# Weight conversion from double to single precision: the sign carried by a Prelu slope in place of two kinds of sign pass

## The chip, the cores and the metric

The kernel runs on one core of one Trainium2 chip. The core has a matrix engine (TensorE, PE in the profile; PEld is its loading of weights), a vector engine (VectorE, DVE), a scalar engine (ScalarE, ACT), GpSimd (POOL) and SyncE (SP), which here does nothing but issue DMAs. The metric is the device time of one execution in microseconds (us). Three runs of the kernel before gave 1497.77 us as the median, 1496.57 and 1499.21 us as the ends.

## The reference, cut to what matters

```python
def _attn_ref(q, k, v, p):
    p_packed = sm_attn(p, k, v)              # 32 packed tokens per head attend to 576
    return sm_attn(q, p_packed, p_packed)    # 576 tokens per head attend to the 32

def _moe_ref(x, w_in, w_out):                # x: 4608 x 512, d_ff 2048
    h = x @ w_in
    g = h - np.tanh(h)
    return (g @ w_out).astype(np.float32)

def _moe2_ref(x, w_in, w_out):
    h = x @ w_in
    g = h * np.cos(h)
    return (g @ w_out).astype(np.float32)

def reference(**kwargs):                     # 8 batches, 8 heads, 576 tokens, width 64
    attn_out = _attn_ref(...)
    x = heads put side by side, one row for each token
    return _moe2_ref(_moe_ref(x, ...), ...)
```

The four weight matrices are double precision (float64). The kernel gets them as 64-bit words and has to make single-precision words of them on the chip. That conversion is all that the change touches.

## The kernel before, in words

**Stages.** There are 8 batches of 576 tokens, handled as 16 half-batches of 288 tokens. The first feed-forward layer with its attention is a row of 128 steps, numbered n = 0 to 127. A step takes two of the 16 column groups of `w_in` for one half-batch: `h1` (L508) does twelve matmuls into a PSUM tile `h`, `el1` and `el2` (L529, L535) compute g = h - tanh(h) on ScalarE and VectorE, `el3` and `el4` split g into a high and a low half, and `ymm1` (L568) multiplies the g of two steps earlier by the `w_out` groups, 24 matmuls. The `h` tile has two buffers, and VectorE's L545 is the last that reads one. Attention of the next batch is spread over the steps as pieces (`early`, `mid`, `quick`), and so is `gmat` with `gsplit` (L470, L489), which multiplies the packed attention rows by converted `w_in` groups and splits the product `g`: the high half on ScalarE (L493), the low half on VectorE (L498). After step 127 there is one 512-token tile of the second layer done plainly (`h2`), and then four passes over pairs of tiles in a scheme with fewer products (`hprod`, `yprod`, L900, L910).

**Weight conversion.** `Conv` (L131 to L253) has three parts. `a` takes a staged tile `st` of 128 x 512 doubles. `hi` is each upper 32-bit word and `x` each lower one. L167 reads `hi` as a single and multiplies it by 2^-112, which leaves the right exponent in the wrong place (three bits too far right). L170 scales the lower word to a small integer. `b` then shifts the word left by three and ors the low bits in (`join`, L208, VectorE). The shift pushes the sign bit out, so the sign has to be put into `x` beforehand, and this is done in one of two ways, read letter by letter from `SPLIT` (first layer) and `SPLIT2` (second layer): for "S" ScalarE writes a half-precision number with the right sign over the upper half of `x` (L175), for "L" VectorE ands the sign out of `hi` and ors it into `x` (L187). `c` splits a converted tile into a high half on ScalarE (L231) and a low half on GpSimd (L232); of the first layer only `w_out` tiles go through it.

**Where the conversions stand.** There are 32 tiles for each layer. The first layer's are converted in the prologue and in steps 0 to 21 (`STEP_A` says how many calls of `a` a step makes); `SPLIT` has 12 "S" and 20 "L". The second layer's are converted in steps 34 to 126 (`CONV2`), all but the last 8 the "S" way.

**Order.** The first part of the prologue (to L1004) and everything from step 15 on stands in a manual schedule, that is in program order. Between them, in steps -16 to 14, Tile's planner orders each engine's queue from the program, by priority and by its own estimate of when things are ready. Loads of staged tiles are issued by `prefetch` (L144) on SP's queue, after a `join` has freed a slot of the pool `wp`.

Of the kernel before, what the change touches and what calls it, by code (L numbers as in the profile page):

```python
# [14 lines left out]
U16 = mybir.dt.uint16  # L15
U32 = mybir.dt.uint32
F16 = mybir.dt.float16
BF16 = mybir.dt.bfloat16
AF = mybir.ActivationFunctionType
ALU = mybir.AluOpType  # L20
# [13 lines left out]
    "i2 i0 i3 i1 o1 o0 i4 i5 i6 i7 o3 o4 o2 o5 o7 i8 "  # L34
    "o6 i9 i10 i11 i14 o9 i12 i13 o8 i15 o11 o13 o12 o10 o15 o14"
).split()
SPLIT = "LLSSLLSLLLSLSLSLLSLSLSLSLLSLLSLL"
SPLIT2 = "S" * 24 + "L" * 8
STEP_A = (1, 2, 2, 2, 1, 2, 1, 1, 1, 1, 0, 2, 1, 1, 1, 1, 1, 1, 0, 3, 1, 1)
CONV2 = (34, 35, 37, 38) + tuple(16 * k + r for k in (3, 4, 5, 6) for r in (0, 2, 3, 5, 6))  # L40
CONV2 += (112, 114, 116, 118, 120, 122, 124, 126)
# [29 lines left out]
    11: (13,), 12: (12, 14), 13: (15, 18, 16), 14: (19,), 16: (17,), 17: (20, 21), 18: (22,),  # L71
}
PREP0 = (23, 24, 25)
SGN = -2147483648
LOW_BIAS = -0.5 + 2.0 ** -10


# [1 line left out]
def fused_kernel(ctx, tc, qT, kT, v, pT, w1i, w1o, w2i, w2o, ident, out):  # L79
    nc = tc.nc  # L80
    B, _, _, _, HB = qT.shape
    S = 2 * HB
# [36 lines left out]
    def f32(ap):  # L119
        return ap.bitcast(F32)  # L120
# [10 lines left out]
    class Conv:  # L131
# [20 lines left out]
        def a(self):  # L152
            self.prefetch()
            if not self.ready:
                return
            kind, f, st = self.ready.pop(0)
            way = self.split[self.na]
            self.na += 1
            if kind == "w1i":
                if f // 2 not in w1in:  # L160
                    w1in[f // 2] = wp.tile([128, 2, 512], F32, tag="w", name="w1i")
                w = w1in[f // 2][:, f % 2, :]
            else:
                w = self.alloc_tmp()
            sv = st.rearrange("p (n two) -> p n two", two=2)
            hi, x = sv[:, :, 1], sv[:, :, 0]
            nc.scalar.activation(out=w, in_=f32(hi), func=AF.Copy, scale=2.0 ** -112)  # L167
            halves = st.bitcast(U16).rearrange("p (n four) -> p n four", four=4)
            if way != "D":
                nc.scalar.activation(  # L170
                    out=x, in_=x.bitcast(U32), func=AF.Identity,
                    scale=2.0 ** -29 * (1 - 2.0 ** -11), bias=LOW_BIAS,
                )
            if way == "S":
                nc.scalar.activation(  # L175
                    out=halves[:, :, 1].bitcast(F16), in_=f32(hi), func=AF.Copy, scale=2.0 ** -60
                )
            self.done_a.append((kind, f, hi, w, x, way))

        def b_ops(self):  # L180
            if not self.done_a:
                return []
            kind, f, hi, w, x, way = self.done_a.pop(0)
            wi = w.bitcast(I32)

            def sign():
                nc.vector.scalar_tensor_tensor(  # L187
                    out=x, in0=hi, scalar=SGN, in1=x, op0=ALU.bitwise_and, op1=ALU.bitwise_or
                )

            def shift():
                nc.vector.tensor_scalar(
                    out=wi, in0=wi, scalar1=3, scalar2=None, op0=ALU.logical_shift_left
                )

            def put_sign():
                nc.vector.scalar_tensor_tensor(
                    out=wi, in0=hi, scalar=SGN, in1=wi, op0=ALU.bitwise_and, op1=ALU.bitwise_or
                )

            def join():
                if way == "D":
                    nc.vector.scalar_tensor_tensor(
                        out=wi, in0=x, scalar=29, in1=wi,
                        op0=ALU.logical_shift_right, op1=ALU.bitwise_or,
                    )
                else:
                    nc.vector.scalar_tensor_tensor(  # L208
                        out=wi, in0=wi, scalar=3, in1=x,
                        op0=ALU.logical_shift_left, op1=ALU.bitwise_or,  # L210
                    )
                if kind == "w1i":
                    self.bdone.add(f)
                else:
                    self.done_b.append((kind, f, w))
                if kind[1] == "2":
                    stores.append((raw[kind[2]][f // 2][:, f % 2], w))
                self.prefetch()

            return {"S": [join], "L": [sign, join], "D": [shift, put_sign, join]}[way]  # L220

        def b(self):
            for fn in self.b_ops():
# [426 lines left out]
    def cos_round(a, h):  # L650
        nc.scalar.activation(out=a, in_=h, func=AF.Identity, bias=MAGIC)

    def cos_frac(a, h):
        nc.vector.scalar_tensor_tensor(
            out=a, in0=a, scalar=MAGIC, in1=h, op0=ALU.subtract, op1=ALU.subtract
        )
# [306 lines left out]

    conv = Conv([("w1" + o[0], int(o[1:])) for o in ORDER], 3, SPLIT, alloc_st, alloc_tmp)

# [74 lines left out]

    conv2 = Conv(todo2, 2, SPLIT2, alloc_st2, alloc_tmp2)

# [25 lines left out]
    for n, (blk, s) in enumerate(steps):  # L1068
# [7 lines left out]
        st = {}  # L1076
# [85 lines left out]
    for s in range(NSTEP):  # L1162
        st = st0 if s == 0 else {}
# [70 lines left out]
    def psp():  # L1234
        i = nbank[0] % 4
        nbank[0] += 1
        if banks[i] is not None:
            t, banks[i] = banks[i], None
            return t
        return psx.tile([128, TB], F32, tag=f"p{i}", bufs=1, name="p")  # L1240
# [78 lines left out]
    for t in pairs:  # L1319
# [23 lines left out]
        for F in range(NSTEP):  # L1343
            w = wfirst if (t, F) == (pairs[0], 0) else None
# [4 lines left out]
            A, C, B = psp(), psp(), psp()  # L1349
# [82 lines left out]
        for k, (p, P) in enumerate(jobs):  # L1432
# [7 lines left out]
            hi, lo = done[k]  # L1440
# [102 lines left out]
```

## Time and profile before

| what | value |
|---|---|
| time, median of 3 runs | 1497.77 us (1496.57 to 1499.21) |
| profiled execution, first to last instruction (span) | 1498.1 us |
| the profiled execution's own time | not given apart from the span; the span lies inside the range of the runs |
| PE busy | 1443.1 us, 96% |
| DVE busy | 1230.8 us, 82% |
| ACT busy | 1034.3 us, 69% |
| POOL busy | 126.6 us, 8% |
| DMA | 307.64 MB, mean 205 GB/s |

Busy times are of one profiled execution. An engine's idle time costs something only where that engine sets the end of its stage, so the table by itself says little: the stages have to be read one by one.

### The profile page before, as it was taken

The page shows a single profiled execution, that of the slowest core. Times are in us where ns is not written, and L with a number is a line of the kernel's source. Part 1 is how long each engine was busy: PE and PEld are TensorE (multiplying, and loading weights), DVE is VectorE, ACT ScalarE, POOL GpSimd, SP SyncE. Part 2 cuts the span into 40 slices and gives each one's busy share as a digit, 9 for nine tenths or more (in the row PEclk, how much of TensorE's full clock was granted, in tenths as well). Part 3 has the DMA queues.
Part 4 walks back from the last instruction along what each step waited for, and adds up shares of the span by engine and source line. Part 5 has one row for each costly group of instructions (what it writes and reads, how often), then busy time and mean ns, then how long its engine had stood idle before and what let it go on. Part 6 is the DMA issues. An engine that isn't in the chain of part 4 may idle for free.

```text
span 1498.1 us, 29038 instructions
## 1 busy us (share of the span) xinstructions
PE 1443.1 (96%) x11296; PEld 1309.5 (87%) x11296; DVE 1230.8 (82%) x1689; ACT 1034.3 (69%) x1592; POOL 126.6 (8%) x102
## 2 busy tenths in 40 slices
PE   4789999999999999999999999999999999999998
PEld 2668888999899899989998888998889888998898
DVE  6999888897988989899986778886888688868874
ACT  5888766879788796887875656655665466636652
POOL 0221101111111112111120000000000000000000
PEclk8799999999999999999999999999999999999999
DMA  9633363645747566473669747787668766777656
GB/s 351 226 122 103 122 210 118 222 138 199 249 140 252 169 210 211 166 245 128 206 257 370 256 159 233 230 256 210 203 188 254 214 207 190 232 240 208 179 162 184
DMA packets 179977, 307.64 MB, mean 205 GB/s; under 512 B 14912, under 2 KB 110144, under 8 KB 179840
## 3 DMA queue, kind: packets, MB, share of 16 engines
q1 hardware_dynamic: 179840, 305.79, 63.2%
q8 instruction: 90, 1.47, 0.4%
q14 instruction: 47, 0.39, 0.1%
HBM read 238.35 MB, written 67.37 MB: 204 GB/s over the span
## 4 chain that ended last, share of the span: by engine, by line
PE 81%; ACT 7%; DVE 5%; issue 3%; DMA 2%; POOL 0%; SPq 0%; DVEq 0%; POOLq 0%; ACTq 0%
PE p L900 21%; PE y L579 20%; PE y L910 14%; PE h L517 10%; PE p L910 6%; PE h L640 3%; PE y L716 3%; PE gp L479 2%; ACT st L175 1%; ACT u L533 1%; DVE y L551 1%; ACT st L170 1%; DMA yw<-wod 1%; DVE d L545 1%; ACT y L539 1%
## 5 line engine op out<-in xcount | busy, mean ns | idle before, releaser
L579 PE MATMUL y<-gh,w1o 128*128 128x288 f32 x2048 | 307.5, 303 | 9.1 <-ACT w1o L231 2.8
L579 PEld LDWEIGHTS y<-gh,w1o 128*128 128x128 f32 x2048 | 280.8, 190 | 38.3 <-ACT t L532 15.3
L900 PE MATMUL p<-b,hw 128*128 128x512 f32 x1302 | 310.4, 391 | 0.0
L900 PEld LDWEIGHTS p<-b,hw 128*128 128x128 f32 x1302 | 239.0, 188 | 47.0
L517 PE MATMUL h<-a,g 128*128 128x288 f32 x1536 | 227.9, 297 | 15.3 <-DVE g L498 7.5
L517 PEld LDWEIGHTS h<-a,g 128*128 128x128 f32 x1536 | 212.7, 190 | 19.1 <-ACT st L170 8.2
L532 ACT ACTIVATE t<-h 128x576 f32<-128x576 f32 x128 | 85.1, 665 | 127.2 <-PE h L517 127.1
L579 PE MATMUL y<-gl,w1o 128*128 128x288 f32 x1024 | 158.5, 297 | 0.0
L579 PEld LDWEIGHTS y<-gl,w1o 128*128 128x128 f32 x1024 | 145.2, 191 | 0.1
L910 PE MATMUL y<-yw,yh 128*128 128x256 f32 x768 | 136.0, 279 | 1.5 <-DMA yw<-wod 1.4
L551 DVE COPY_PREDICATED y<-k,t 128x576 f32<-128x576 int16 x128 | 111.7, 873 | 10.8 <-DVE y L547 0.5
L544 DVE TENSOR_TENSOR t<-h,t 128x576 f32<-128x576 f32 x128 | 95.2, 744 | 29.9 <-ACT u L533 28.9
L910 PEld LDWEIGHTS y<-yw,yh 128*128 128x128 f32 x768 | 117.5, 188 | 2.5 <-ACT o L921 2.0
L564 DVE TENSOR_TENSOR gl<-y,gh 128x576 fp32r<-128x576 f32 x128 | 107.0, 836 | 1.7 <-ACT gh L559 1.6
L910 PE MATMUL y<-yw,yl 128*128 128x256 f32 x384 | 107.3, 279 | 0.0
L918 DVE TENSOR_TENSOR yl<-k,yh 128x1024 fp32r<-128x1024 f32 x72 | 87.0, 1219 | 23.5 <-ACT yh L921 22.9
L547 DVE SCALAR_TENSOR_TENSOR y<-y,d 128x576 f32<-128x576 f32 x128 | 97.0, 758 | 2.4 <-ACT y L539 2.1
L559 ACT ACTIVATE gh<-y 128x576 fp32r<-128x576 f32 x128 | 87.8, 686 | 12.2 <-DVE y L551 11.6
L545 DVE TENSOR_TENSOR d<-u,h 128x576 f32<-128x576 f32 x128 | 95.0, 742 | 0.0
L910 PE MATMUL y<-yw,gh 128*128 128x256 f32 x512 | 94.0, 280 | 0.0
L910 PE MATMUL p<-yw,yh 128*128 128x256 f32 x512 | 91.0, 279 | 0.0
L921 ACT ACTIVATE c<-p 128x512 f32<-128x512 f32 x96 | 56.9, 593 | 49.2 <-PE p L900 49.2
(164 smaller groups left out, 2580.6 us busy)
## 6 DMA issues: line engine op xcount, KB each, us to landing
yw<-wso SPq DMA_DIRECT2D x128, 256.0 KB, 3.1
hw<-wsi SPq DMA_DIRECT2D x124, 256.0 KB, 3.1
w1i<-w1d SPq DMA_DIRECT2D x48, 512.0 KB, 5.1
yw<-wod SPq DMA_DIRECT2D x96, 256.0 KB, 3.3
hw<-wid SPq DMA_DIRECT2D x93, 256.0 KB, 3.3
y<-ye SPq DMA_DIRECT2D x80, 144.0 KB, 1.9
st<-w1i SPq DMA_DIRECT2D x16, 512.0 KB, 8.4
v<-vv SPq DMA_DIRECT2D x16, 512.0 KB, 6.5
```

What stands on the lines that cost most here:

```text
L517: nc.tensor.matmul(out=h[:, x, 0:HB], lhsT=gw[b, f // 4, half][:, ga, c0:c0 + 128], rhs=a2[b, half][:, aa, HB * j:HB * j + HB], start=(n = ...
L532: nc.scalar.activation(out=st["t"], in_=h, func=AF.Tanh)
L544: lambda: nc.vector.tensor_tensor(out=t, in0=hs, in1=t, op=ALU.subtract),
L545: lambda: nc.vector.tensor_tensor(out=d, in0=u, in1=hs, op=ALU.mult),
L547: lambda: nc.vector.scalar_tensor_tensor(out=y, in0=y, scalar=PC0 - PC1 * PC1 / (4 * PC2), in1=d, op0=ALU.add, op1=ALU.mult,),
L551: lambda: nc.vector.copy_predicated(out=y, mask=k.bitcast(I16), data=t),
L559: nc.scalar.activation(out=st["gh"], in_=st["g"], func=AF.Copy)
L564: nc.vector.tensor_tensor(out=st["gl"], in0=st["g"], in1=f32(st["gh"]), op=ALU.subtract)
L579: nc.tensor.matmul(out=yps[blk][d][:, 0:HB], lhsT=w1out[f][:, wh, 128 * d:128 * d + 128], rhs=st[gg][:, x, :], start=(s in first and x == ...
L900: nc.tensor.matmul(out=dst, lhsT=w[:, wi, 128 * j:128 * j + 128], rhs=b[j][bi], start=(first and n == 0), stop=(n == 5), skip_group_check= ...
L910: nc.tensor.matmul(out=dst[m // 2][:, 256 * (m % 2):256 * (m % 2) + 256], lhsT=src[:, 128 * m:128 * m + 128], rhs=w[:, wi, :], start=(firs ...
L918: nc.vector.tensor_tensor(out=out, in0=x, in1=y, op=op)
```

## The change

The multiplication at L167 becomes a Prelu with the same scale and with a slope of 2^32 for negative numbers. A negative word thus gets an exponent larger by 32, and that bit of the exponent field is the one that the later shift by three moves into the place of the sign. So no sign has to be put into `x`: the half-precision write on ScalarE (L175) and the and-or on VectorE (L187) are gone, and every tile is converted by L167, L170 and the join. All 32 + 32 tiles take this way (letter "A"); another way, "V", is defined and not used. The low half of `g` (L498) stays on VectorE. Nothing else is edited: `STEP_A`, `CONV2`, the order of tiles, the pools and the loads are as they were.

```diff
-SPLIT = "LLSSLLSLLLSLSLSLLSLSLSLSLLSLLSLL"
-SPLIT2 = "S" * 24 + "L" * 8
+SPLIT = "A" * 32
+SPLIT2 = "A" * 32
...
             hi, x = sv[:, :, 1], sv[:, :, 0]
-            nc.scalar.activation(out=w, in_=f32(hi), func=AF.Copy, scale=2.0 ** -112)
-            halves = st.bitcast(U16).rearrange("p (n four) -> p n four", four=4)
-            if way != "D":
+            nc.scalar.activation(
+                out=w, in_=f32(hi), func=AF.Prelu, scale=2.0 ** -112, alpha=2.0 ** 32
+            )
+            if way == "A":
                 nc.scalar.activation(
                     out=x, in_=x.bitcast(U32), func=AF.Identity,
                     scale=2.0 ** -29 * (1 - 2.0 ** -11), bias=LOW_BIAS,
                 )
-            if way == "S":
-                nc.scalar.activation(
-                    out=halves[:, :, 1].bitcast(F16), in_=f32(hi), func=AF.Copy, scale=2.0 ** -60
-                )
...
-            def sign():
-                nc.vector.scalar_tensor_tensor(
-                    out=x, in0=hi, scalar=SGN, in1=x, op0=ALU.bitwise_and, op1=ALU.bitwise_or
-                )
...
-            return {"S": [join], "L": [sign, join], "D": [shift, put_sign, join]}[way]
+            return {"A": [join], "V": [shift, join]}[way]
```

## Rows read from the trace of the kernel before

**Rows 1.** The page: busy time of each engine, and slices of the span.
```profile
PE 1443.1 (96%) x11296; PEld 1309.5 (87%) x11296; DVE 1230.8 (82%) x1689; ACT 1034.3 (69%) x1592; POOL 126.6 (8%) x102
...
PE   4789999999999999999999999999999999999998
```

**Rows 2.** Windows by stage: length, busy PE, PEld, DVE, ACT, POOL; granted clock, DMA.
```profile
14.00:35.00 21.00, 9.20 (x162) 4.03 (x154) 17.80 (x35) 14.68 (x24) 0.00 (x0) 0.77 1.04 394
35.00:110.00 75.00, 60.39 (x513) 49.06 (x514) 69.67 (x106) 66.19 (x114) 21.08 (x14) 0.84 0.55 188
110.00:172.00 62.00, 57.73 (x546) 53.21 (x546) 55.56 (x80) 54.06 (x101) 9.58 (x7) 0.99 0.37 117
172.00:700.00 528.00, 518.08 (x5027) 481.04 (x5027) 460.88 (x739) 411.74 (x719) 77.43 (x61) 1.00 0.56 189
700.00:800.00 100.00, 99.02 (x683) 95.10 (x682) 82.69 (x111) 76.04 (x134) 18.16 (x14) 1.00 0.64 227
```

**Rows 3.** Windows, VectorE's sign pass L187 alone: length, busy time and count.
```profile
14.00:35.00 21.00, 1.38 (x2) 0.77 1.04 394
35.00:110.00 75.00, 12.22 (x14) 0.84 0.55 188
110.00:172.00 62.00, 4.49 (x4) 0.99 0.37 117
```

**Rows 4.** Windows, ScalarE's sign pass L175 alone: length, busy time and count.
```profile
35.00:110.00 75.00, 10.92 (x8) 0.84 0.55 188
110.00:172.00 62.00, 2.79 (x2) 0.99 0.37 117
172.00:700.00 528.00, 33.23 (x24) 1.00 0.56 189
```

**Rows 5.** The chain that ended at 172 us, from 14 us: shares by line.
```profile
by line: issue 12.4%; PE y L579 8.8%; DVE y L551 6.9%; PE h L517 6.3%; ACT st L175 5.8%; ACT st L170 4.0%; DVE st L187 3.8%; DVE t L544 3.1%; ACT gh L559 2.9%; DVE d L545 2.5%; PE gp L479 2.4%; ACT w1i L167 2.4%; ACT y L539 2.2%; ACT u L533
```

**Rows 6.** Groups of ScalarE, 14 to 172 us: busy, mean ns, idle before.
```profile
L175 ACT ACTIVATE st<-st 128x512 f16<-128x512 f32 x12 | 16.4, 1368 | 0.1
...
L532 ACT ACTIVATE t<-h 128x576 f32<-128x576 f32 x20 | 13.1, 657 | 10.3 <-PE h L517 10.3
L542 ACT ACTIVATE k<-u 128x576 bf16<-128x576 f32 x19 | 13.1, 689 | 0.0
...
L167 ACT ACTIVATE w1i<-st 128x512 f32<-128x512 f32 x16 | 10.7, 683 | 0.0
```

**Rows 7.** Timeline of VectorE near 37 and 88 us: start, duration, line.
```profile
36.70 0.69 DVE L187 SCALAR_TENSOR_TENSOR st<-st 128x512 int32<-128x512 int32 x1
37.30 0.16 DVE L349 RECIPROCAL sm<-sm 128x1 f32<-128x1 f32 x1
...
88.40 1.47 DVE L187 SCALAR_TENSOR_TENSOR st<-st 128x512 int32<-128x512 int32 x1
89.79 0.74 DVE L544 TENSOR_TENSOR t<-h,t 128x576 f32<-128x576 f32 x1
```

**Rows 8.** Timeline of GpSimd near 88 us.
```profile
87.74 1.58 POOL L407 TENSOR_TENSOR u<-u,m 128x576 f32<-128x576 f32 x1 [5.24 <-DVE m L406]
```

**Rows 9.** Waits of TensorE, 35 to 110 us: total, times, longest, us.
```profile
PE h L517 <- DVE g L498: 7.3, 1, 7.3
PE gp L479 <- DVE w1i L208: 3.7, 2, 2.1
```

**Rows 10.** Waits of TensorE, 14 to 35 us.
```profile
PE pt L458 <- DVE px L388: 0.8, 1, 0.8
```

**Rows 11.** Waits of TensorE, 172 to 700 us.
```profile
PE h L517 <- DVE d L545: 3.6, 4, 0.9
```

**Rows 12.** Timeline of ScalarE near 376 us: start, duration, line.
```profile
376.46 1.37 ACT L175 ACTIVATE st<-st 128x512 f16<-128x512 f32 x1
377.57 0.74 ACT L532 ACTIVATE t<-h 128x576 f32<-128x576 f32 x1
```

**Rows 13.** Line L1133: the later of the two table loads of ScalarE (ns).
```profile
L1133 ACT ACT_TABLE_LOAD  x1: 1283/1283/1283, 778.5 to 778.5; - x1
```

More of the change, by code (lines that the diff above doesn't have):

```diff
@@ L73 @@
 PREP0 = (23, 24, 25)
-SGN = -2147483648
 LOW_BIAS = -0.5 + 2.0 ** -10
@@ L194, in shift @@
                 )
[L196 to L199, printed above, removed]
             def join():
-                if way == "D":
+                if way == "V":
                     nc.vector.scalar_tensor_tensor(
```

## The prediction, made before the changed kernel was run

> **What bounds the kernel now.** I read the page first. TensorE is busy 96% of the span and its slices stand at 9 nearly everywhere, but the first three are 4, 7 and 8 [rows 1]. So the kernel is bound by TensorE but for its first 110 us or so, and 32 of the 64 conversions lie there. The windows by stage show what bounds each stretch [rows 2]. From 14 to 35 us and from 35 to 110 us VectorE is the fullest engine (17.80 of 21 us and 69.67 of 75 us), ScalarE is close behind (66.19 of 75), and TensorE has time to spare (60.39 of 75, and part of that at a granted clock of 0.84). From 110 to 172 us all three are nearly full: TensorE 57.73 of 62, so that at most 4.3 us can be won there. From 172 to 700 us TensorE is busy 518.08 of 528 us, and from 700 to 800 us 99.02 of 100: there a pass that is taken from another engine is worth something only where TensorE waits for it. The chain of waits up to 172 us names both passes that the change removes: of its 158 us ScalarE's L175 holds 5.8%, that is 9.2 us, and VectorE's L187 holds 3.8%, 6.0 us [rows 5]. Together 15.2 us: with both gone this chain is that much shorter, and something else may then be late.
>
> **The change part by part.**
>
> *The multiplication as a Prelu.* The trace before has no Prelu. The nearest rows are ScalarE's other functions: in the same stretch Tanh (L532) takes 657 ns and Relu (L542) 689 ns on 576 columns, the copy of L167 itself 683 ns on 512 strided ones [rows 6]. These three differ by 5%, so I take 683 ns, no change. The upper end is the dearest pass of this size, L175 with 1368 ns [rows 6], the lower end the 657 ns of Tanh, 0.03 us a tile less. The Trainium skill, "ScalarE: Activation LUTs", section "Table sets: the hidden batching unit", says that functions come in sets and that a function out of the loaded set needs a table load; its list of the cheap functions that are in every set names relu, copy, identity and abs, and not Prelu. The trace agrees on what one load costs, 1283 ns [rows 13], and shows nothing on Prelu's set. By that rule's bad case the change loses; it is the last rival below.
>
> *ScalarE's sign pass L175.* Twelve stand before 172 us and 24 later [rows 4, 6]. One takes 1.37 us, but the next instruction starts 1.11 us after it [rows 12]; so 1.1 us of ScalarE's time each.
>
> *VectorE's sign pass L187.* 20 stand before 172 us (2, 14 and 4 in the three stretches), 8 after 700 us, where TensorE is full [rows 2, 3]. An undisturbed one holds the queue for 0.60 us (36.70 to 37.30) [rows 7]. The mean is 0.91 us, 18.09 us over 20 [rows 3], since some are much longer: the one at 88.40 takes 1.47 us, and GpSimd's pass from 87.74 to 89.32 lies over most of it [rows 7, 8]. Of such a one I count 0.60 us, since the next pass may have to sit out the same collision. The upper end, all that L187 was busy, stays for the range. The Trainium skill, "SBUF — State Buffer", section "Who interferes with whom", has it that a VectorE instruction with two SBUF inputs and a GpSimd instruction that reads SBUF lock each other out for a whole instruction. By that rule the excess stays whenever the next pass has two such inputs, and goes where it has one (L544 behind the pass at 88.40 reads PSUM); the sum by the rule lies between 8.4 and 12.2 us for the stretch below.
>
> *14 to 35 us.* The prologue's order is manual. TensorE's transpose of the packed rows waits 0.8 us for `px` on VectorE [rows 10], and ahead of `px` stand a sign pass and its join. Gain 0.6 us, one pass; bounds 0 and 0.8. The rest of this stretch is attention on VectorE, which the change doesn't touch.
>
> *35 to 110 us.* VectorE sets the pace: 5.3 us idle of 75 [rows 2]. Fourteen passes by 0.60 us make 8.4 us. ScalarE gets rid of 8 by 1.1 us, 8.8 us, so it doesn't take VectorE's place. TensorE's two long waits here end with VectorE (7.3 us for the low half of `g`, 3.7 us for a join) [rows 9], which fits. Upper bound 12.2 us [rows 3]; lower bound 3 us, the sign passes ahead of the waited-for joins (five of 0.60 us, an estimate), where the planner or the attention chain of the next batch holds the rest. I take 8.4 us: what bounds the stretch loses that much of its queue.
>
> *110 to 172 us.* Four passes of VectorE and two of ScalarE go (2.4 and 2.2 us), TensorE's idle time is 4.3 us [rows 2 to 4]. I take half of the latter, 2.1 us; bounds 0 and 4.3.
>
> *172 to 700 us.* TensorE waits 3.6 us in all for L545, four times 0.9 us [rows 11]. L545 comes behind Tanh on ScalarE, which at 377.57 starts 1.11 us late because an L175 stands ahead of it [rows 12]. The passes gone, Tanh starts up to 1.1 us sooner, and 1.1 is more than 0.9. Gain 3.6 us; bounds 0 (if another wait of the same length stands behind) and 3.6. All else that leaves ScalarE here (24 by 1.1 us) is covered by TensorE, and so are VectorE's 8 passes after 700 us: 0 us, at most the 1.0 us that TensorE is idle there [rows 2].
>
> No DMA, no wait and no buffer is added; staged tiles come free sooner, so their loads go out sooner.
>
> *The sum.* 0.6 + 8.4 + 2.1 + 3.6 = 14.7 us. The span is 1498.1 us, so 1483.4 us; the median of the runs is 0.3 us below the span, so 1483.1 us for the metric. As a cross-check: the first three terms make 11.1 us of the 15.2 us that the chain holds.
>
> **The rivals.**
>
> *The early order keeps part of it.* In steps -16 to 14 the planner lays out the queues anew, and the attention of the next batch passes through VectorE, GpSimd and ScalarE in turn. If that chain sets the pace, the lower bounds hold: 0 + 3 + 1 + 3.6 = 7.6 us, so about 1490 us. For it: 12.4% of the chain up to 172 us is "issue", not work [rows 5]. Against it: VectorE is busy 93% of 35 to 110 us [rows 2].
>
> *All of it comes through.* Collisions leave with the passes, and TensorE fills its gaps: 0.8 + 12.2 + 4.3 + 3.6 + 1.0 = 21.9 us, about 1476 us. Against it: TensorE would have to have no wait at all from 110 us on.
>
> *The loads take over.* The DMA engines are full from 14 to 35 us (share 1.04, 394 GB/s) [rows 2]. If the tiles arrive no sooner than now, the terms up to 110 us are gone, 9.0 us, and 1492 us is left. Against it: from 35 to 110 us the share is 0.55.
>
> *A Prelu that costs more, and the kernel is slower.* ScalarE gets back 12 by 1.1 us, 13.2 us, before 172 us and does 32 Prelus there: it breaks even at 0.41 us more for each, about 1.09 us in all. At L175's 1368 ns it has 32 by 0.69 us, 21.9 us, more and is the bound in place of VectorE: 8.7 us more than before, of which its idle time covers a part, so some 1500 us. If each Prelu switched the table and back, 64 loads by 1.28 us are 82 us; the 13.2 us and ScalarE's idle time of 23.0 us from 14 to 172 us [rows 2] cover 36, and it would be about 1540 us. Against it: the similar cost of three functions [rows 6].
>
> **How the numbers follow.** Forecast (14.7 us, its own range 1479 to 1487) 0.59; early order 0.20; all of it 0.11; loads 0.05; dear Prelu 0.05. The range takes in the second and third: 1476 to 1491.5 us. What a measurement of this kernel can tell from no change is 0.2%, 3.0 us. Forecast and first three rivals all lie more than that below; to fall within 3.0 us the early stages would have to give nothing and the four waits also to stay, for which I take 0.05 out of the first two rivals' share. Faster 0.90, same 0.05, slower 0.05.
>
> **What would show it.** Right: L167 at some 0.68 us, no table load but two; the start of the steady stretch (now 172 us) 9 to 13 us earlier, by VectorE's shorter queue; the four waits for L545 gone; from 800 us on the same length. Wrong: the steady stretch starts where it did, with VectorE idle more than now in 35 to 110 us (then order or loads bound it), or the waits for L545 remain, or L167 is longer.

## The result, and the profile after

The changed kernel takes 1479.46 us (median, 1478.96 to 1480.42); beside it the kernel before took 1497.89 us. The ratio is 0.9875, 95% interval 0.9861 to 0.9889: 18.4 us less, where 14.7 had been forecast. 1483.1 us was predicted, with a range of 1476.0 to 1491.5.

The page of the changed kernel, busy times and the slices of TensorE:

```profile
PE 1434.7 (97%) x11296; PEld 1305.6 (88%) x11296; DVE 1211.8 (82%) x1661; ACT 992.6 (67%) x1556; POOL 127.1 (9%) x102
...
PE   5889999999999999999999999999999999999998
```

VectorE has 28 instructions less and ScalarE 36, exactly the sign passes, and the first three slices of TensorE stand at 5, 8 and 8 instead of 4, 7 and 8 [rows 1]. The windows by stage, columns as in [rows 2]:

```profile
14.00:35.00 21.00, 9.91 (x157) 4.49 (x149) 17.59 (x35) 13.37 (x24) 0.00 (x0) 0.77 1.04 394
35.00:110.00 75.00, 63.66 (x581) 55.52 (x580) 67.78 (x103) 65.25 (x122) 22.95 (x15) 0.91 0.60 211
110.00:172.00 62.00, 59.38 (x599) 54.93 (x598) 52.16 (x79) 49.63 (x94) 9.61 (x7) 1.00 0.34 108
172.00:700.00 528.00, 522.33 (x5049) 486.81 (x5048) 469.97 (x749) 392.45 (x711) 77.71 (x62) 1.00 0.57 192
700.00:800.00 100.00, 100.00 (x631) 93.09 (x630) 75.04 (x99) 70.67 (x115) 16.49 (x13) 1.00 0.75 275
```

From 35 to 110 us VectorE and ScalarE are about as full as before, but the same 75 us hold 581 matmuls instead of 513: the work got denser, not lighter. From 110 us on TensorE's idle time shrinks in each window.

The functions of ScalarE up to the steady stretch (busy us, mean ns, idle before), where L166 is the Prelu:

```profile
L518 ACT ACTIVATE t<-h 128x576 f32<-128x576 f32 x20 | 13.0, 652 | 12.7 <-PE h L503 12.6
L528 ACT ACTIVATE k<-u 128x576 bf16<-128x576 f32 x19 | 13.0, 682 | 0.0
...
L166 ACT ACTIVATE wt<-st 128x512 f32<-128x512 f32 x16 | 10.8, 673 | 1.0 <-DMA st<-w1o 0.9
L166 ACT ACTIVATE w1i<-st 128x512 f32<-128x512 f32 x16 | 10.7, 680 | 0.0
```

A Prelu takes 673 to 680 ns, the copy took 683 [rows 6]. The table loads in the whole span are the two of before:

```profile
L953 ACT ACT_TABLE_LOAD x1 | 1.3, 1283 | 0.7 <-PEq L1519 0.7
L1119 ACT ACT_TABLE_LOAD x1 | 1.3, 1283 | 0.0
```

TensorE's waits from 172 to 700 us:

```profile
PE y L565 <- DVE ye L595: 2.3, 1, 2.3
PE sc L303 <- PE h L503: 1.8, 5, 0.8
PE s L303 <- PE h L503: 1.3, 6, 0.2
PE pt L444 <- DVE g L484: 0.2, 1, 0.2
```

The line that answers to [rows 11], four waits for L545 (now L531), is gone. At the place of [rows 12], Tanh no longer stands behind a sign pass; it waits for TensorE instead:

```profile
361.24 0.69 ACT L170 ACTIVATE st<-st 128x512 int32<-128x512 uint32 x1
362.64 0.65 ACT L518 ACTIVATE t<-h 128x576 f32<-128x576 f32 x1 [0.71 <-PE h L503]
```

Where the time went can be read off the starts of the 128 steps (first matmul of `h1`). The table gives how much earlier a step starts than in the profile before, in us:

| run | step 0 | step 10 | step 17 | step 31 | step 104 | step 127 | end of span |
|---|---|---|---|---|---|---|---|
| after | 1.2 | 9.8 | 11.6 | 13.1 | 18.6 | 18.7 | 19.5 |
| prelu_only | 0.2 | -0.3 | 0.5 | 2.0 | 1.8 | 1.8 | 3.2 |
| no_vector_sign | 0.5 | 4.5 | 5.4 | 5.4 | 5.2 | 5.2 | 7.9 |
| no_scalar_sign | 1.7 | 1.5 | 2.2 | 2.3 | 7.7 | 7.8 | 9.1 |
| second_layer_only | 0.8 | 0.8 | 0.7 | 0.7 | 6.1 | 6.2 | 9.1 |

The last column holds noise of its own. After the steps TensorE meets up to three waits for loads and stores in the last passes, which differ from profile to profile (0.8 and 0.5 us for loads and 0.6 us for ScalarE in the one after, 0.6 and 0.8 us for loads in the one before, one of 0.2 us in prelu_only). A run's own time is 1.8 us above its span (1480.42 against 1478.6 us for the profiled run after), so the profile before, with 1498.1 us, is of a run about 2 us above the median: of the 19.5 us between the two spans about 1 is the choice of runs.

### The profile page after: what moved, and what is told of

Read it like the earlier page. It is cut to its first block, busy times and chain, and to the rows that moved or that the text cites. A ratio compares the mean times of both kernels' runs of the same rounds, so it can differ in the third digit from the quotient of the medians.

```text
span 1478.6 us, 29015 instructions
## 1 busy us (share of the span) xinstructions
PE 1434.7 (97%) x11296; PEld 1305.6 (88%) x11296; DVE 1211.8 (82%) x1661; ACT 992.6 (67%) x1556; POOL 127.1 (9%) x102
## 4 chain that ended last, share of the span: by engine, by line
PE 88%; DVE 5%; issue 3%; ACT 2%; DMA 1%; POOL 1%; SPq 0%; DVEq 0%; POOLq 0%; ACTq 0%
PE y L565 24%; PE p L886 21%; PE y L896 15%; PE h L503 12%; PE p L896 6%; PE h L626 3%; PE y L702 3%; PE gp L465 2%; DMA yw<-wod 1%; DVE y L537 1%; PE pp L364 1%; DVE t L530 1%; DVE y L533 1%; PE sc L303 1%; PE tp L341 1%
## 5 line engine op out<-in xcount | busy, mean ns | idle before, releaser
L545 ACT ACTIVATE gh<-y 128x576 fp32r<-128x576 f32 x128 | 87.9, 687 | 11.3 <-DVE y L537 9.1
L531 DVE TENSOR_TENSOR d<-u,h 128x576 f32<-128x576 f32 x128 | 95.0, 742 | 0.0
```

The lines of the kernel that those rows point to most:

```text
L531: lambda: nc.vector.tensor_tensor(out=d, in0=u, in1=hs, op=ALU.mult),
L545: nc.scalar.activation(out=st["gh"], in_=st["g"], func=AF.Copy)
```

## The experiments

### One kind of pass at a time

The changed kernel gets back one kind of pass, or both, on the tiles that had it before. The Prelu stays in all four, and a pass then sets a sign that is already there.

```diff
-            if way == "A":
+            if way != "V":
...
+            if way == "S":
+                halves = st.bitcast(U16).rearrange("p (n four) -> p n four", four=4)
+                nc.scalar.activation(
+                    out=halves[:, :, 1].bitcast(F16), in_=f32(hi), func=AF.Copy, scale=2.0 ** -60
+                )
...
+            def sign():
+                nc.vector.scalar_tensor_tensor(
+                    out=x, in0=hi, scalar=-2147483648, in1=x, op0=ALU.bitwise_and, op1=ALU.bitwise_or
+                )
...
-            return {"A": [join], "V": [shift, join]}[way]
+            return {"A": [join], "S": [join], "L": [sign, join], "V": [shift, join]}[way]
...
 prelu_only:        SPLIT, SPLIT2 as before
 no_vector_sign:    as before, each "L" an "A"
 no_scalar_sign:    as before, each "S" an "A"
 second_layer_only: SPLIT as before, SPLIT2 = "A" * 32
```

**prelu_only.** 

> Only L167 becomes a Prelu; both kinds of sign pass stay on the tiles that had them (they set a sign that is already there), and each engine's order of instructions is that of before. Theory (a Prelu costs what the copy cost, the gain is all from the passes that go): L167 at some 0.68 us, no table load but two, 1497.9 us within 1.5. Rival (the Prelu has a price of its own that the changed kernel hides): L167 over 0.75 us or more table loads, and over 1500 us.

1498.12 us beside 1497.38, ratio 1.0005 (0.9996 to 1.0015). The Prelu takes 670 to 680 ns, and there are two table loads. The Prelu costs nothing that shows; all of the gain is from the passes that go. This profile also tells how far two profiles of the same order stray: 0.5 us at step 17, 1.5 more at step 31 (the clock, see the last section). Other pairs stray further: the changed kernel and evac_first (below), in which VectorE, ScalarE and GpSimd do the same up to step 28, differ by 1.2 us at step 17 (11.6 and 10.4 us ahead of before), and gl8_evac_first and evac_loads_kept by 0.9. So a difference of about 1 us between two single profiles shows nothing by itself.

**no_vector_sign.** 

> The changed kernel with ScalarE's sign pass put back on the 12 + 24 tiles that had it; VectorE's 20 + 8 passes are gone. Theory (VectorE's queue sets the pace up to 110 us, ScalarE's passes cause the four waits from 172 to 700 us): most of the early gain is here, 8 to 10 us by 172 us, 0.85 us at the end of the steps, and the four waits of 0.9 us stay; about 1488 us. Rival (ScalarE's passes set the early pace): at most 4 us by 172 us, about 1494 us.

1492.31 us, ratio 0.9966 (0.9953 to 0.9978): 5.1 us. Between the two: 4.5 us at step 10 and 5.4 at step 17, less than the 8 to 10 of the theory and more than the 4 of the rival. The window from 35 to 110 us shows why (VectorE is the third engine, ScalarE the fourth):

```profile
35.00:110.00 75.00, 61.15 (x542) 52.63 (x543) 64.83 (x98) 68.88 (x119) 21.07 (x15) 0.89 0.56 201
```

ScalarE, 66.19 of 75 us before [rows 2], is now at 68.88 and the fullest. It has taken VectorE's place. The four waits are there as they were:

```profile
PE h L513 <- DVE d L541: 3.7, 4, 0.9
```

The way from step 127 to the second layer's first matmul is 9.47 us before and 7.96 here.

**no_scalar_sign.** 

> The changed kernel with VectorE's sign pass put back on the 20 + 8 tiles that had it; ScalarE's 12 + 24 passes are gone. Theory: 2 to 3 us by 172 us, the four waits for VectorE's L545 of before gone (5 us with the small ones beside them), the two waits of 0.5 us at the end of the steps stay; about 1490.5 us. Rival (ScalarE's passes set the early pace): 8 us or more by 172 us and about 1484 us.

1490.38 us, ratio 0.9959 (0.9944 to 0.9973): 7.0 us. 2.2 us at step 17, none of the four waits, and the way behind step 127 at 9.47 us: as the theory had it. From 35 to 110 us VectorE stays the fullest, and ScalarE is at 57.43:

```profile
35.00:110.00 75.00, 58.54 (x520) 49.02 (x520) 66.98 (x105) 57.43 (x106) 21.79 (x14) 0.87 0.53 186
```

**second_layer_only.** 

> Only the second layer's 32 tiles lose their sign passes; the first layer keeps both kinds (its multiplication is a Prelu too). The planner's order up to step 14 is that of before. Theory (the parts add up): no gain by 172 us; 5.0 us from 172 to 700 us and 0.85 us at the end of the steps, so 1492.0 us, or 1490.5 us if the granted clock doesn't fall behind the wait after step 30 as it did before. Rival (the late gain follows from the early one): less than 3 us in all, over 1495 us.

1490.40 us, ratio 0.9955 (0.9940 to 0.9970): 7.0 us. By the trace, 5.5 us between steps 17 and 127 and 1.5 us behind step 127, nothing before; the late part doesn't depend on the early one. The 0.85 us of the expectation for the last passes was too little.

Up to step 17 the single removals give 5.4 and 2.2 us, together 7.6; both at once give 11.6.

### Is it the order of the planner?

In steps -16 to 14 the planner lays the queues out anew for each variant, so part of the 11.6 us could be a lucky order.

```diff
 before_from_4, after_from_4 (of the kernel before, of the changed one):
-STEP_ORDERED = 15
+STEP_ORDERED = 4
 token_passes (prelu_only, each sign pass on one column):
-                    out=halves[:, :, 1].bitcast(F16), in_=f32(hi), func=AF.Copy, scale=2.0 ** -60
+                    out=halves[:, 0:1, 1].bitcast(F16), in_=f32(hi)[:, 0:1], func=AF.Copy, scale=2.0 ** -60
...
-                    out=x, in0=hi, scalar=-2147483648, in1=x, op0=ALU.bitwise_and, op1=ALU.bitwise_or
+                    out=x[:, 0:1], in0=hi[:, 0:1], scalar=-2147483648, in1=x[:, 0:1], op0=ALU.bitwise_and, op1=ALU.bitwise_or
```

**before_from_4.** 

> The kernel before with its manual order from step 4 on instead of step 15: the planner orders only steps -16 to 3. It is the pair of after_from_4. Alone: no theory of its size, 1495 to 1510 us, since the program order of steps 4 to 14 isn't tuned.

1511.12 us, ratio 1.0089 (1.0068 to 1.0111), 1.1 us above the range.

**after_from_4.** 

> The changed kernel with its manual order from step 4 on; steps 4 to 14 have the same order as in before_from_4 but for the passes that are gone. Theory (shorter queues on VectorE and ScalarE give the early gain, whichever way the queues are laid out): 10 to 13 us less than before_from_4 at the start of step 17, 17 to 20 us less in all. Rival (the planner's new order gave the part that the single removals do not add up to, 3.6 us): at most 8 us at step 17, 15 us in all.

1492.51 us, 18.6 us less than its pair. Its steps start earlier than the pair's by 2.4 us at step 4, 8.0 at step 10, 14.4 at step 17 and 19.7 at step 127. From step 4 to 17, where the order is written out and the same in both but for the passes (and joins on VectorE that move up by a place or two where a sign pass stood), 12.1 us are won. Somewhat above the expected 10 to 13 at step 17, and far from the rival's 8: the gain needs no new order.

**token_passes.** 

> Both kinds of sign pass stay in their places on the tiles that had them, on one column of the 512 each (they do not make the sign any more, the Prelu does). The planner lays this out in a third way. Theory (time in the queue counts): 20 + 12 short passes by 0.06 to 0.2 us, 3 us in all at most, are left of the early price, so 8 to 11 us at step 17 and 1480 to 1484 us. Rival (the order of after is a lucky one): 6 us or less at step 17, over 1486 us.

1484.16 us, ratio 0.9910 (0.9893 to 0.9927); 7.6 us at step 17. That is just outside what the theory allowed and not the rival's number. It is 4.0 us behind the changed kernel at step 17, where short passes were to cost 3 at most. But they were not as short as the expectation took them to be (up to 165 us; busy, mean ns, idle before):

```profile
L176 ACT ACTIVATE st<-st 128x1 f16<-128x1 f32 x12 | 2.5, 208 | 0.1
L188 DVE SCALAR_TENSOR_TENSOR st<-st 128x1 int32<-128x1 int32 x20 | 5.7, 295 | 1.4 <-ACT st L170 1.4
```

On VectorE the median of all 28 is 0.15 us and the longest takes 1.19 us. Up to the start of step 19 VectorE is busy 133.35 us here and 128.88 us in the changed kernel, 4.5 us more. So the 4.0 us can be the price of the passes and need no order. This run does not show that an order is worth anything; how much of the 11.6 us is due to it stays open.

That holds for the single removals as well. VectorE has 213 instructions up to step 20 that are not sign passes; 200 of them keep the order of before in no_scalar_sign, 172 in the changed kernel and 157 in no_vector_sign. So it is not shown that 5.4 and 2.2 us make less than 11.6 by the passes alone.

### Versions that go on from there

In the cuts of code below the step numbers 14 and 29 stand for named constants of the kernels.

**gl_on_gpsimd.** The low half of g = h - tanh(h) of the first 14 steps on GpSimd.

```diff
-            nc.vector.tensor_tensor(
+            e = nc.gpsimd if st["n"] < 14 else nc.vector
+            e.tensor_tensor(
                 out=st["gl"], in0=st["g"], in1=f32(st["gh"]), op=ALU.subtract
```

> The changed kernel with the low half of g = h - tanh(h) of steps 0 to 13 (14 passes, 0.75 us each on VectorE) on GpSimd. Theory (VectorE still sets the pace up to 110 us, 67.8 of 75 us): its queue is 10.5 us shorter, collisions with GpSimd's longer passes (1.4 us each) take back half, so 3 to 5 us faster than the changed kernel, about 1475.5 us. Rival (the collisions and GpSimd's longer way to ymm1 take all): 1479 us or more.

1481.05 us, ratio 0.9892 (0.9875 to 0.9909): no gain, the rival's outcome. Against the changed kernel it is 1.4 us ahead at step 10 and 1.1 us behind at step 17, both about what profiles of one order stray by.

**et_on_scalar.** Two copies of 0.69 us from VectorE to ScalarE.

```diff
-            if b != 1:
+            if True:
                 nc.scalar.activation(out=et[:, 0:4, :], in_=tv, func=AF.Copy)
```

> The changed kernel with the two copies of transposed scores of the second batch (0.68 us each) on ScalarE instead of VectorE. Theory (VectorE is still the fuller of two engines that set the early pace together): 0.5 to 1.5 us faster by step 17, 1478.5 us. Rival (ScalarE is as full by now): no gain or a loss by 1 us, 1479.5 to 1480.5 us.

1482.46 us (1479.63 to 1483.76), ratio 0.9896 (0.9879 to 0.9912). 0.2 us ahead of the changed kernel at step 17: no gain that shows, as the rival had it, and a median above its 1480.5. Both engines were near full in the changed kernel (67.78 and 65.25 us of 75).

**evac_first.** TensorE's largest wait left, 2.3 us for L595 behind step 30, comes from VectorE's order in step 29.

```diff
-        for fn in mid[n]:
-            fn()
+        if n != 29:
+            for fn in mid[n]:
+                fn()
...
             if hs == NSTEP - 1:
                 yevac1(hb)
+        if n == 29:
+            for fn in mid[n]:
+                fn()
```

> The changed kernel, but in step 29 VectorE evacuates the finished output tile (L595, four passes) ahead of the low halves of g and the transpose instead of behind them. Theory (TensorE's wait of 2.3 us behind step 30, which the change left as it was, is VectorE's order there, and the fall of the granted clock seen behind it in some profiles is its consequence): the wait shrinks to 0.5 us or less and no clock of 0.5 stands near 225 us; 1.8 us faster than the changed kernel in its undisturbed case, up to 3.4 us against one with the fall; about 1477.5 us. Rival (the low halves of g are now late and stop TensorE later in the step): 1479.5 us or more.

1481.31 us, ratio 0.9889 (0.9873 to 0.9906): the time of the rival, but by neither of the two reasons. The wait for L595 went from 2.3 to 0.5 us, but TensorE's waits from 172 to 700 us begin with a new one:

```profile
PE gp L466 <- DMA w1i<-w1d: 2.5, 2, 1.7
```

SyncE's queue (start, duration, line) in this kernel:

```profile
223.65 2.92 SPq L605 DMA_DIRECT2D y<-ye  x4
226.66 0.88 SPq L455 DMA_DIRECT2D w1i<-w1d  x2
```

and in the changed one:

```profile
205.76 1.52 SPq L454 DMA_DIRECT2D w1i<-w1d  x2
...
224.33 3.22 SPq L604 DMA_DIRECT2D y<-ye  x4
```

`mid` also issues loads. Moved behind the evacuation, they stood behind its stores, which wait for VectorE, and went out 21 us later. This was my oversight: a step that is moved takes its DMAs along.

**gl8_evac_first.** As evac_first, with the GpSimd passes of gl_on_gpsimd in steps 0 to 7 alone.

> evac_first with the low half of g = h - tanh(h) on GpSimd in steps 0 to 7 alone. In gl_on_gpsimd the gain over the changed kernel was 1.4 us at step 10 and turned into a loss of 1.1 us by step 17. Theory (the loss comes from the passes of steps 8 to 13, where TensorE sets the pace and GpSimd's longer way is seen): 1.4 us kept, about 1476 us. Rival (collisions take it whatever the steps): as evac_first or slower.

1480.81 us, ratio 0.9890 (0.9875 to 0.9909). The time is the rival's. At step 17 it is 1.0 us ahead of the changed kernel and 2.3 us ahead of evac_first, where the theory had 1.4; with a stray of 1.2 us the size is not shown. What there was is lost to a wait of 3.4 us for the same loads.

**evac_loads_kept.** As gl8_evac_first, with step 29's loads in their old place (`loads29` takes them out of `mid[29]`; that part of the edit is left out here).

```diff
-        if n != 29:
-            for fn in mid[n]:
-                fn()
+        for fn in loads29 if n == 29 else mid[n]:
+            fn()
```

> gl8_evac_first with the loads that step 29 issues (two tiles of w_in for step 31, v of the next batch) left in their old place on SP's queue, ahead of the stores of the evacuated tile. In evac_first these loads were issued behind the stores, and TensorE's products with w_in in step 31 waited 2.5 us for them, which neither theory there had named. Theory (SP's order is all that went wrong): the 1.9 us from the shorter wait behind step 30 and the 1.0 us of steps 0 to 7 are both kept after step 32, no wait for w1i, no clock of 0.5 after 200 us; about 1477 us. Rival (another wait takes its place): 1479.5 us or more.

1477.17 us (1475.87 to 1479.31), ratio to the kernel before 0.9866 (0.9848 to 0.9884), the theory's time. Ahead of the changed kernel by 1.9 us at step 17 and 3.5 at step 31; 1.1 us go to another wait of TensorE, in step 32, whose cause the list below (its waits from 172 to 700 us) does not name, and 2.4 us are left at step 127. With strays of up to 1.2 us the 1.9 at step 17 is known only roughly; the 1.6 us between steps 30 and 31 are the wait that got shorter. It is faster than the kernel before; against the changed one the median is 2.3 us lower, but the two intervals overlap.

```profile
PE sc L305 <- issue: 1.1, 1, 1.1
PE y L568 <- ACT t L520: 0.7, 1, 0.7
```

## Why the prediction was right, step by step, and where not

**The Prelu at the copy's price: right.** 673 to 680 ns, and prelu_only is at 1.0005. The last rival is out, and the bad case that it took from the Trainium skill, "ScalarE: Activation LUTs", section "Table sets: the hidden batching unit", does not occur: no load beyond two.

**0.60 us for a pass of VectorE, the collisions staying: right.** Windows from 0 to the start of step 19, before and in no_vector_sign (VectorE is the third engine):

```profile
0.00:169.29 169.29, 131.62 (x1209) 106.78 (x1210) 142.65 (x222) 137.37 (x242) 31.00 (x27) 0.90 0.56 194
0.00:163.92 163.92, 129.66 (x1210) 106.18 (x1211) 130.65 (x203) 136.81 (x242) 29.70 (x27) 0.95 0.57 201
```

VectorE is busy 12.0 us less: 20 by 0.60, although the 20 passes were busy 18.1 us [rows 3]. With ScalarE's passes gone on both sides (no_scalar_sign and the changed kernel) it is 140.05 and 128.88 us, 11.2 us less. The exact 0.60 is partly luck, since no_scalar_sign, which keeps all 20 passes, is itself 2.6 us below before. In the stretch 15 of VectorE's instructions take more than 0.9 us before, by 10.0 us in all, and 13 in no_vector_sign, by 9.8 us: the long passes did not go with the sign passes, others are long in their place. Each of these 28 lies over an instruction of GpSimd for 0.5 to 2.0 us, so the collisions fell on the passes behind. The Trainium skill, "SBUF — State Buffer", section "Who interferes with whom", states that a VectorE instruction with two SBUF inputs contends with a GpSimd instruction that reads SBUF. The trace agrees: none of the 28 reads PSUM, and the joins, 9 of the 13, have two SBUF inputs.

**14 to 35 us: 0.6 forecast, 1.2 measured** at the start of step 0. Within what two profiles differ by. The wait for `px` is gone here and in no_vector_sign; in no_scalar_sign 0.6 us of it stays.

**35 to 110 us: 8.4 forecast, 8.6 measured** (1.2 at step 0, 9.8 at step 10), by reasoning that was half wrong. The step that failed is that VectorE by itself bounds the stretch. With VectorE's passes alone gone, steps 0 to 10 gain 4.1 us and ScalarE is the fullest engine; with ScalarE's alone gone they gain nothing (1.7 us at step 0, 1.5 at step 10). Before, the two are 93% and 88% busy, 3.5 us apart, and VectorE's removal was worth little more than that distance. What I wrote in passing, that ScalarE loses 8.8 us as well and so doesn't take VectorE's place, was the condition of the whole term. That both limit the stretch is how I read these runs; the new orders of the queues are not separated from it.

Two of the supports were read wrongly. The wait of 7.3 us that I cited from [rows 9] ends at the start of step 0, at 35.6 us, so it lies almost wholly ahead of the stretch, and it is still 7.3 us in the changed kernel; only the waits for the join there got shorter, from 3.7 to 1.0 us. And the chain gave both passes a share, ScalarE's the larger [rows 5], while VectorE's removal alone gave more: a share of the chain was no price.

**110 to 172 us: 2.1 forecast, 1.8 measured** (steps 10 to 17).

**172 to 700 us: 3.6 forecast, 5.5 measured.** The mechanism was right: the four waits go with ScalarE's passes and stay with VectorE's. The term was mis-sized, since I took the list of waits at its word: each of the four steps begins 1.07 us sooner, not 0.91, and three other steps (50, 66, 98) begin 0.2 to 0.3 us sooner, delays that stand in no line of that list that I counted. Together these make 5.1 us; the rest is smaller shifts.

**Behind 700 us: 0 forecast, 1.5 measured.** VectorE's last eight passes were put down as covered, with 1.0 us of TensorE's idle time as the bound. Without them the way from step 127 to the second layer's first matmul is 7.96 instead of 9.47 us: 9.47 in all four profiles with such passes there, 7.96 in all ten others (in token_passes with one-column ones). The cover was not there: VectorE itself was busy 18.10 of 20 us from 740 to 760 us. Before, the sign pass at 762.25 us stands ahead of a join that takes 1.80 us, where the same join takes 0.69 us in no_vector_sign; measured from the start of step 127, L551 starts at -0.25 us instead of -1.96, and TensorE then waits twice 0.5 us for the high half of g behind it.

**Not in the sum: 1.5 us of clock** between steps 30 and 31, which the change didn't cause (next section but one). Without it the parts make 1.2 + 8.6 + 1.8 + 5.5 + 1.5 = 18.6 us, beside 18.4 between the medians. What the forecast lacked is in the two late terms, 1.9 and 1.5 us.

Of the rivals, "all of it" came nearest in time (1476) and not in its reason: TensorE still waits 2.3 us at one place, and the collisions stayed. The early order and the loads did not take the gain (the 7.6 us of the first were not its lower bounds, as it said: those of 110 to 172 and 172 to 700 us were 0, which leaves 3 us and some 1495); a wait of ScalarE for a load is in the profile, 0.9 us in all.

## What to carry to other kernels

Where two engines are both near 90% busy and hand work to each other, expect from a removal on one of them little more than the distance to the other, and don't add up what single removals give: here the distance was 3.5 us in 75 and the gain 4.1, and up to step 17 the gains were 5.4 and 2.2 us alone, 11.6 together (10.4 by the profile of evac_first). It is one kernel, and its queues were laid out anew each time, so this is a thing to try and not a rule. A pass that is "covered" by a full engine needs that engine to be full at that very place, so read the steps at the seam of two stages one by one. And when a group of operations is moved, list its DMAs first.

## What the runs showed of the hardware that I had not expected

TensorE's granted clock falls behind a wait of some 2.3 us, in some executions and not in others. The wait for the evacuation behind step 30 (L609 before, L595 in the changed kernel) is the same in the profiles before and after (2.31 and 2.32 us). In the one before, the window around it has a granted clock of 0.70, so part of it at the lower of the two levels (1.2 GHz instead of 2.4):

```profile
235.00:240.00 5.00, 3.98 (x20) 4.01 (x21) 4.90 (x10) 2.41 (x4) 1.44 (x1) 0.70 0.34 109
```

and the sixteen matmuls behind the wait take 3.34 us:

```profile
236.02 3.34 PE L579 MATMUL y<-gh,w1o 128*128 128x288 f32 x16 [2.31 <-DVE ye L609]
```

In the changed kernel's profile the clock stays at 1.00, and the same sixteen take 2.37 us:

```profile
223.00:228.00 5.00, 3.55 (x27) 3.58 (x28) 5.00 (x10) 2.76 (x5) 1.45 (x1) 1.00 0.29 92
```

```profile
224.45 2.37 PE L565 MATMUL y<-gh,w1o 128*128 128x288 f32 x16 [2.32 <-DVE ye L595]
```

The fall costs 1.5 us (prelu_only, with the order of before and no fall, is 1.5 us further ahead at step 31 than at step 30). Of the 13 profiles with a wait of 1.7 us or more in this place (in evac_first and gl8_evac_first it is the wait for loads in step 31), 9 have the fall and 4 have not; in evac_loads_kept, whose waits there are 0.7 and 1.1 us, the clock stays at 1.00. That the length of the wait decides is likely by that, and not shown: it is one profile. What decides between fall and no fall at the same wait stays open, and with it 1.5 us in any single run of these kernels.
